# First units of a fused attention, mixing and expert kernel: weights converted 512 columns at a time with a mask made on POOL

## The chip, the cores and the metric

The kernel runs on one core of a Trainium2 chip. TensorE (PE) does the matrix products, VectorE (DVE), ScalarE (ACT) and GpSimd (POOL) the elementwise work, and SyncE (SP) issues most loads. The metric is device time in microseconds; the time before is the median of three executions. The rows shown come from one profiled execution.

## The reference

Three layers follow one another; the weights of the second arrive as 64-bit floats.

```python
# 1. attention in chunks of 64: q, k, v are (8, 8, 576, 64)
attn = softmax(scale * q_c @ k_c.T); x = attn @ v_c          # -> (8, 576, 512)
# 2. channel mixing
xk = mu_k * x + (1.0 - mu_k) * x_prev                        # x_prev: x one token earlier
xr = mu_r * x + (1.0 - mu_r) * x_prev
k = np.maximum(xk @ w_k, 0.0)                                # w_k (512, 1024), float64
v = k * k @ w_v                                              # w_v (1024, 512), float64
r = 1.0 / (1.0 + np.exp(-(xr @ w_r)))                        # w_r (512, 512), float64
x = r * v
# 3. four causal attention experts, two of them chosen per token by a gate
```

## The kernel before, in words

Each float32 operand of a product is split in a high and a low part, and each product is three matmuls (`mm3`, L51 to L59). The first two layers (`attn_mix`) go over 12 units of 384 tokens. Of a unit, PE does 48 matmuls for r (`mix_r`), 96 for k (`mix_k`), 96 for v (`mix_v`). Between them stand the steps of attention (`attend`): transposes of q and k (L126), scores `Sps` (L153), softmax on DVE and ACT (L158 to L167), transposes of the probabilities, and `PVps` (L183). One block of scores covers two tiles of 128 tokens.

**Conversion.** The weights are read as pairs of 32-bit words (`st`) and turned into float32 by shifts and masks: `conv`, 256 columns at a time, 40 pieces: 8 of w_r, 16 of w_k, 16 of w_v. For a piece SP issues a load of 256 KB; ACT squares the high word read as a float (L297, to find values too small); DVE runs L298, L299, L300, and with L302 multiplies by the outcome of the comparison; then `split` copies the high part on ACT (L314) and POOL subtracts (L315) for the low part. There are three buffers `st`, two of `cb`, two of `cz`.

**Shift.** For each unit and each 128 channels, `s_shift` builds xr and xk: POOL takes the difference of a token and the one before (L226), DVE multiplies and adds (L235), ACT copies the high part (L236), and the low part (L237) is a subtraction, on POOL in units 0 and 1 and on DVE later.

**What sets the order.** The functions are called in an order written out by hand (`CFG["first"]`, `CFG["pro"]`, `CFG["early"]`); a list scheduler then fixes the order on each engine, and each engine takes its instructions in that order. All 40 pieces are converted while the first unit is worked on. In the third layer (`experts`) nothing is edited.

Of the kernel before, what the change touches and what calls it, by code (L numbers as in the profile page):

```python
# [8 lines left out]
F32 = mybir.dt.float32  # L9
# [13 lines left out]
CFG = dict(ps=(2, 3, 1, 2), P=5, sm=3, load=6, lag=(3, 4), out=(5, 1), qk1=(1, 1), qk0=(10, 1.2), v=(11, 1), order=(3, 4, 0, 1, 2), after=1, conv='v', clo='g', x2hi='g', x2lo='v', ylo='g', yhi='v', xt='aa', r2='av', klo='vg', slo='gv', d='gg', amul='vg', nearly=2, x2b=1, yb=4, qb=4, direct=((0, 1), (1, 1), (1, 1)), tailAV=4, kp=1, yt=1, yf=2, zb=1, om=(4, 3, 2, 1, 0), hp=1000, x2d=2, early=3, rate0=0.43, rate=0.45, sh=(10, 12, 2), sh2=(11, 1, -1), pro=(17, 0.56, 20, 14), alag=2, seq=0, end=2, outL=(10, 2), outE=2, first='qqcvcvcv', kcp='aa', dsc='v', ldb=2, vb=3, cn=256, stb=3, xb=4, pa=5, tb=2, first_j=7, cb=2)  # L23
# [10 lines left out]
def eng(nc, c):  # L34
    return nc.vector if c == "v" else nc.gpsimd
# [26 lines left out]
def attn_mix(tc, at, x2T, q, k, v, mu_k, mu_r, w_k, w_v, w_r, ident, attended_all, mixed_k):  # L62
# [14 lines left out]
    with ExitStack() as ctx:  # L77
# [12 lines left out]
        mu = wkr.tile([128, 2, KD], F32, name="mu")  # L90

# [51 lines left out]
        def s_S(j):  # L143
# [19 lines left out]
            z = at.tile([128, 2 * H], F32, tag="z", name="z")  # L163
# [3 lines left out]
            eng(nc, CFG["amul"][2 * j // TPU >= CFG["nearly"]]).tensor_tensor(  # L167
# [53 lines left out]
        def s_shift(u, ws, g):  # L221
            x = XT[u]
            now, prev = x[:, g, :, 1:], x[:, g, :, :SEG]
            late = u >= CFG["nearly"]
            d = wkr.tile([128, NSEG, SEG], F32, tag="xa", bufs=2, name="xa")
            eng(nc, CFG["d"][late]).tensor_tensor(d, now, prev, op=ALU.subtract)  # L226
            for w in ws:
                nm = "kr"[w]
                if g == 0:
                    XS[u, w] = Split(wkr.tile([128, KD, UNIT], F32R, tag="xh" + nm, name="xh" + nm),  # L230
                                     wkr.tile([128, KD, UNIT], F32R, tag="xl" + nm, name="xl" + nm))
                o = XS[u, w]
                a = d if w == ws[-1] else wkr.tile([128, NSEG, SEG], F32, tag="r2", bufs=2, name="xb")
# [126 lines left out]
        for c in CFG["first"] + "q" * (CFG["ldb"] - 2) + "v" * (CFG["vb"] - 3):  # L360
# [9 lines left out]
        steps, rate, rest, at0 = CFG["pro"]  # L370
        credit = 0.0
        for i in range(steps):
            attend(2)
            credit += rate
            while credit >= 1:
# [4 lines left out]
        convert(rest)  # L380
        if steps <= at0:
            attended(0)
            first_shift()
# [29 lines left out]
def expert_weights(tc, at, w_gate, wq, wk, wv):  # L413
# [467 lines left out]
```

## Time and profile before

| | |
|---|---|
| three runs | 1073.24 us median (1073.1 to 1078.78) |
| profiled execution | 1074.6 us, of which the span of the trace is 1072.8 us |
| PE busy over the span | 1004.7 us (94%) |
| DVE, ACT, POOL busy | 749.8, 586.0, 448.0 us |
| PE busy in the first five of 40 slices | 4, 6, 7, 8, 6 tenths |
| DVE busy in the same slices | 4, 9, 9, 9, 9 tenths |

A slice is 26.8 us. A busy digit is the share of a slice; 9 is 90% or more. After the sixth slice PE is at 9 but for the end. The duration of one instruction holds its own waiting inside the engine, and neighbours on one engine overlap by some tens of nanoseconds, so sums of durations slightly exceed the time covered.

### The profile page before, as it was taken

How to read it: one execution, taken by the hardware profiler on the slowest of the kernel's cores; microseconds unless marked ns; L12 is line 12 of the kernel's file. 1: busy time of each engine (PE TensorE's matmuls, PEld its weight loads, DVE VectorE, ACT ScalarE, POOL GpSimd, SP SyncE). 2: the span in 40 equal slices, each digit the busy share in tenths (PEclk: the TensorE clock that was granted, in tenths of full speed). 3: DMA queues.
4: the chain of work that ended last, by engine and by line, in shares of the span. 5: the costliest groups of instructions: out<-in, count | busy, mean ns of one | idle time of the engine just before them, and what ended most of it. 6: DMA issues, size and time to landing. Idle time of an engine off the chain costs nothing.

```text
span 1072.8 us, 22466 instructions
## 1 busy us (share of the span) xinstructions
PE 1004.7 (94%) x8422; PEld 959.2 (89%) x8422; DVE 749.8 (70%) x1853; ACT 586.0 (55%) x1413; POOL 448.0 (42%) x550
## 2 busy tenths in 40 slices
PE   4678689999999999999999999999999999999997
PEld 3567579999899999999999999999999898999985
DVE  4999984562765665575666542498787687878996
ACT  4647547254454535464534323367776666766674
POOL 1485652453654555464644544534331233323101
PEclk9779799999999999999999999999999999999999
DMA  8735462223333232424021222662642535254212
GB/s 190 197 93 139 120 165 53 59 57 84 79 90 90 70 85 60 115 59 119 22 70 40 69 60 63 136 175 60 156 143 64 161 71 165 64 154 123 83 53 71
DMA packets 170404, 105.29 MB, mean 98 GB/s; under 512 B 133832, under 2 KB 146232, under 8 KB 170296
## 3 DMA queue, kind: packets, MB, share of 16 engines
q1 hardware_dynamic: 134904, 54.56, 20.4%
q0 software_dynamic: 35392, 49.30, 17.8%
q8 instruction: 67, 1.10, 0.5%
q14 instruction: 41, 0.34, 0.1%
HBM read 66.01 MB, written 28.38 MB: 88 GB/s over the span
## 4 chain that ended last, share of the span: by engine, by line
PE 64%; DVE 21%; DMA 5%; ACT 4%; issue 4%; SPq 2%; POOL 1%; ACTq 0%; DVEq 0%; POOLq 0%
PE mps L57 12%; PE mps L59 12%; PE mps L58 12%; PE pj L57 5%; PE pj L58 4%; PE pj L59 4%; PE Tps L656 3%; PE AVps L680 2%; PE Tps L126 2%; DVE cb L299 2%; DVE xa L235 2%; PE AVps L676 2%; PE Sps L596 2%; PE Sps L595 2%; DVE cz L302 2%
## 5 line engine op out<-in xcount | busy, mean ns | idle before, releaser
L57 PE MATMUL mps<-kh,wvh 128*128 128x384 f32 x384 | 131.8, 347 | 8.4 <-ACT wvh L314 7.3
L57 PE MATMUL mps<-xhk,wkh 128*128 128x384 f32 x384 | 132.9, 346 | 2.8 <-ACT r L257 2.8
L226 POOL TENSOR_TENSOR xa<-XT 128x384 f32<-128x384 f32 x96 | 95.1, 999 | 88.8 <-DVE xlr L237 46.8
L58 PE MATMUL mps<-kl,wvh 128*128 128x384 f32 x384 | 129.5, 339 | 2.1 <-POOL kl L266 2.1
L58 PE MATMUL mps<-xlk,wkh 128*128 128x384 f32 x384 | 130.3, 339 | 0.0
L59 PE MATMUL mps<-xhk,wkl 128*128 128x384 f32 x384 | 130.0, 339 | 0.0
L59 PE MATMUL mps<-kh,wvl 128*128 128x384 f32 x384 | 128.9, 340 | 0.2
L264 DVE TENSOR_TENSOR r<-r 128x384 f32<-128x384 f32 x80 | 68.6, 858 | 83.1 <-ACT r L257 83.0
L266 POOL TENSOR_TENSOR kl<-r,kh 128x384 fp32r<-128x384 f32 x80 | 87.8, 1102 | 82.1 <-ACT kh L265 81.1
L608 ACT ACTIVATE P<-sm,nm 128x128 f32<-128x128 f32 (+4 forms) x160 | 91.3, 571 | 35.4 <-DVE nm L598 20.1
L235 DVE SCALAR_TENSOR_TENSOR xa<-xa,mu,XT 128x384 f32<-128x384 f32 x96 | 85.8, 907 | 15.1 <-POOL xa L226 15.1
L598 DVE CUSTOM_DVE_ANT_0 sm<-Sps,mask 128x192 f32<-128x192 f32 (+3 forms) x192 | 83.6, 438 | 15.5 <-PE Sps L596 13.7
L265 ACT ACTIVATE kh<-r 128x384 fp32r<-128x384 f32 x96 | 50.3, 524 | 62.2 <-DVE r L264 61.8
L656 PE MATMUL Tps<-ident,P 128*128 128x128 f32 x480 | 81.0, 273 | 2.3 <-DVE P L617 0.9
L57 PEld LDWEIGHTS mps<-kh,wvh 128*128 128x128 f32 x384 | 72.8, 190 | 11.1 <-ACT wvh L314 8.4
L517 POOL DMA_DIRECT2D K<-Kp x64 | 34.1, 546 | 111.6 <-ACT Kp L510 111.0
L57 PE MATMUL mps<-xhr,wrh 128*128 128x384 f32 x192 | 67.3, 353 | 11.5 <-ACT sig L250 4.6
L57 PEld LDWEIGHTS mps<-xhk,wkh 128*128 128x128 f32 x384 | 73.2, 191 | 4.1 <-ACT r L257 3.6
L58 PEld LDWEIGHTS mps<-kl,wvh 128*128 128x128 f32 x384 | 73.1, 190 | 3.4 <-POOL kl L266 3.3
L59 PEld LDWEIGHTS mps<-kh,wvl 128*128 128x128 f32 x384 | 72.6, 190 | 1.2 <-POOL wvl L315 1.0
L58 PEld LDWEIGHTS mps<-xlk,wkh 128*128 128x128 f32 x384 | 73.1, 190 | 0.1
L59 PEld LDWEIGHTS mps<-xhk,wkl 128*128 128x128 f32 x384 | 72.9, 190 | 0.0
(197 smaller groups left out, 2939.7 us busy)
## 6 DMA issues: line engine op xcount, KB each, us to landing
x2T<-x2d POOLq DMA_DIRECT2D x48, 384.0 KB, 3.4
x<-x2T POOLq DMA_DIRECT2D x32, 576.0 KB, 6.1
ldv<-in_v_dram SPq DMA_DIRECT2D x144, 64.0 KB
K<-Kp POOLq DMA_DIRECT2D x64, 144.0 KB, 3.0
ldq<-in_q_dram SPq DMA_DIRECT2D x32, 256.0 KB
ldk<-in_k_dram SPq DMA_DIRECT2D x32, 256.0 KB
out_dram<-o SPq DMA_DIRECT2D x32, 256.0 KB
st<-in_moe_w_k_dram SPq DMA_DIRECT2D x16, 256.0 KB
```

What stands on the lines that cost most here:

```text
L57: nc.tensor.matmul(out=out, lhsT=ah, rhs=bh, start=first and i == 0, stop=False)
L58: nc.tensor.matmul(out=out, lhsT=ah, rhs=bl, start=False, stop=False)
L59: nc.tensor.matmul(out=out, lhsT=al, rhs=bh, start=False, stop=last and i == n - 1)
L226: eng(nc, CFG["d"][late]).tensor_tensor(d, now, prev, op=ALU.subtract)
L235: nc.vector.scalar_tensor_tensor(a, d, mu[:, w, g:g + 1], prev, op0=ALU.mult, op1=ALU.add)
L264: eng(nc, CFG["r2"][u >= CFG["nearly"]]).tensor_tensor(r2, r, r, op=ALU.mult)
L265: nc.scalar.activation(out=o.hi, in_=r2, func=ACTF.Copy)
L266: eng(nc, CFG["klo"][u >= CFG["nearly"]]).tensor_tensor(o.lo, r2, f32(o.hi), op=ALU.subtract)
L517: nc.gpsimd.dma_start(out=d[half[j]], in_=t[half[i]])
L598: nc.vector.tensor_tensor_reduce(out=sm[:n, a:a + w], in0=pp[:n, :w], in1=mk[:, a:a + w], op0=ALU.add, op1=ALU.min, scale=-scale, scalar=3e38,
L608: nc.scalar.activation(out=x[:n, :nk], in_=sm[:n, :nk], func=ACTF.Exp, scale=-1.0, bias=nm[:n, :1], accum_out=z)
L656: nc.tensor.transpose(pp[:, j - j0], x[:, o:o + 128], ident)
```

## The change

Weights go through in 20 pieces of 512 columns (`cn=512`), 4 of w_r, 8 of w_k, 8 of w_v, 512 KB each. The comparison moves to POOL, which turns the square into a word that is zero or a mask (one `tensor_scalar` with one tensor operand); DVE's first instruction ands it in, so three DVE instructions remain, and the buffer `cb` goes. The low part of the weights is subtracted on DVE (`clo='v'`). There are two buffers `st` instead of three; the first four pieces use the not yet used buffers of the shifted x. In units 0 to 2 (`dact=3`) ACT computes (1 - mu) * x_prev, DVE adds mu * x, and DVE also subtracts the low part; POOL takes differences from unit 3 on. The normalising multiplication of the softmax (`amul`) stays on DVE for score blocks 0 to 6, where it was 0 to 2. The order of stages becomes `first='qqcvvcc'`, `pro='aaacaaaaacccaaaaaasacc'` (a: a step of attention, c: a piece, s: the first shift), `early=(2, 1)`. `vb` goes from 3 to 2, and the expert weights take other buffers that have come free; of the three `st` buffers one held such a weight, so the output tiles, which share the tag, had two and have two.

```diff
@@ s_shift
-            late = u >= CFG["nearly"]
-            d = wkr.tile([128, NSEG, SEG], F32, tag="xa", bufs=2, name="xa")
-            eng(nc, CFG["d"][late]).tensor_tensor(d, now, prev, op=ALU.subtract)
+            by_act = u < CFG["dact"]
+            if not by_act:
+                d = wkr.tile([128, NSEG, SEG], F32, tag="xa", bufs=2, name="xa")
+                nc.gpsimd.tensor_tensor(d, now, prev, op=ALU.subtract)
...
-                nc.vector.scalar_tensor_tensor(a, d, mu[:, w, g:g + 1], prev, op0=ALU.mult, op1=ALU.add)
+                m = mu[:, w, g:g + 1]
+                if by_act:
+                    nc.scalar.activation(out=a, in_=prev, func=ACTF.Copy, scale=mu1[:, w, g:g + 1])
+                    nc.vector.scalar_tensor_tensor(a, now, m, a, op0=ALU.mult, op1=ALU.add)
+                else:
+                    nc.vector.scalar_tensor_tensor(a, d, m, prev, op0=ALU.mult, op1=ALU.add)
                 nc.scalar.activation(out=o.hi[:, g], in_=af, func=ACTF.Copy)
-                eng(nc, CFG["slo"][late]).tensor_tensor(o.lo[:, g], af, f32(o.hi[:, g]), op=ALU.subtract)
+                nc.vector.tensor_tensor(o.lo[:, g], af, f32(o.hi[:, g]), op=ALU.subtract)
@@ conv
-            st = at.tile([128, n, 2], I32, tag="st", bufs=CFG["stb"], name="st")
+            i = done[0] - 1
+            if i < 4:
+
+                st = wkr.tile([128, n, 2], I32, tag=("xhr", "xlr", "xhk", "xlk")[i], name="st")
+            else:
+                st = at.tile([128, n, 2], I32, tag="st", bufs=CFG["stb"], name="st")
...
-            b = at.tile([128, n], I32, tag="cb", bufs=CFG["cb"], name="cb")
             z = at.tile([128, n], F32, tag="cz", bufs=2, name="cz")
+            b = z.bitcast(I32)
+
             nc.scalar.activation(out=z, in_=f32(h), func=ACTF.Square)
-            nc.vector.tensor_scalar(b, h, 3, 0x3FFFFFF8, op0=ALU.logical_shift_left, op1=ALU.bitwise_and)
+            nc.gpsimd.tensor_scalar(z, z, F64_SMALL * F64_SMALL, 2.0 - 2.0 ** -20, op0=ALU.is_ge, op1=ALU.mult)
+            nc.vector.scalar_tensor_tensor(b, h, 3, b, op0=ALU.logical_shift_left, op1=ALU.bitwise_and)
             nc.vector.scalar_tensor_tensor(b, l, 29, b, op0=ALU.logical_shift_right, op1=ALU.bitwise_or)
             nc.vector.scalar_tensor_tensor(b, h, -(1 << 30), b, op0=ALU.bitwise_and, op1=ALU.bitwise_or)
-            if nth(CFG["conv"], done[0]) == "v":
-                nc.vector.scalar_tensor_tensor(z, z, F64_SMALL * F64_SMALL, f32(b), op0=ALU.is_ge, op1=ALU.mult)
...
             split(z, dst, g, c0, n)
```

On DVE, early in the program, where w_r's and w_k's pieces alternate with the softmax of the second block of scores (`cb`, `cz`: a piece; `m`, `z`, `P`: the softmax). Before:

```order
L298 TENSOR_SCALAR cb<-st 128x256 x2
L299 SCALAR_TENSOR_TENSOR cb<-st,cb 128x256 x2
L300 SCALAR_TENSOR_TENSOR cb<-st,cb 128x256 x2
L302 SCALAR_TENSOR_TENSOR cz<-cz,cb 128x256 x2
L298 TENSOR_SCALAR cb<-st 128x256
L299 SCALAR_TENSOR_TENSOR cb<-st,cb 128x256
L300 SCALAR_TENSOR_TENSOR cb<-st,cb 128x256
L302 SCALAR_TENSOR_TENSOR cz<-cz,cb 128x256
L158 TENSOR_REDUCE m<-Sps 128x8 x2
```

Now, at the same place (L312 to L314 are the three instructions of a piece, L324 its low part):

```order
L312 SCALAR_TENSOR_TENSOR cz<-st,cz 128x512
L313 SCALAR_TENSOR_TENSOR cz<-st,cz 128x512
L314 SCALAR_TENSOR_TENSOR cz<-st,cz 128x512
L312 SCALAR_TENSOR_TENSOR cz<-st,cz 128x512
L324 TENSOR_TENSOR wrl<-cz,wrh 128x512
L313 SCALAR_TENSOR_TENSOR cz<-st,cz 128x512
L314 SCALAR_TENSOR_TENSOR cz<-st,cz 128x512
L159 TENSOR_REDUCE m<-Sps 128x8 x2
```

A piece of 512 columns is three conversions and one subtraction on DVE, and the conversion of the next piece starts ahead of the subtraction of the last. Up to the last piece DVE has 80 such instructions, where it had 160 of 256 columns.

On POOL, over the conversion of w_r and the first pieces of w_k. Before:

```order
L315 TENSOR_TENSOR wrl<-cz,wrh 128x256 x8
L214 MEMSET XT 128x4
L217 COPY XT<-XT 128x4
L315 TENSOR_TENSOR wkl<-cz,wkh 128x256 x3
L226 TENSOR_TENSOR xa<-XT 128x384 x2
L217 COPY XT<-XT 128x4
L315 TENSOR_TENSOR wkl<-cz,wkh 128x256
L237 TENSOR_TENSOR xlr<-xa,xhr 128x384
```

Now (L311 makes the mask; COPY moves the last token of a unit, and waits for the attention):

```order
L311 TENSOR_SCALAR cz<-cz 128x512 x7
L215 MEMSET XT 128x4
L218 COPY XT<-XT 128x4
L311 TENSOR_SCALAR cz<-cz 128x512 x2
L218 COPY XT<-XT 128x4
L311 TENSOR_SCALAR cz<-cz 128x512 x2
L218 COPY XT<-XT 128x4
L311 TENSOR_SCALAR cz<-cz 128x512 x5
```

All instructions with two tensor operands are gone from POOL here; 20 masks have come.

On PE, at the end of v of unit 0, where it takes the last piece of w_v (`mps` with its number is one bank of 384 results; `kh_1367` before and `kh_1102` now are the last of eight blocks of k). Before:

```order
L57 MATMUL mps_1482<-kh_1367,wvh_91 128x384
L58 MATMUL mps_1482<-kl_1368,wvh_91 128x384
L57 MATMUL mps_1530<-kh_1367,wvh_91 128x384
L58 MATMUL mps_1530<-kl_1368,wvh_91 128x384
L126 MATMUL Tps_2467<-ident_60,ldq_2068 128x128 x4
L126 MATMUL Tps_2474<-ident_60,ldk_2070 128x128 x4
L59 MATMUL mps_1482<-kh_1367,wvl_92 128x384
L59 MATMUL mps_1530<-kh_1367,wvl_92 128x384
```

Now:

```order
L57 MATMUL mps_1187<-kh_1102,wvh_91 128x384
L58 MATMUL mps_1187<-kl_1103,wvh_91 128x384
L59 MATMUL mps_1187<-kh_1102,wvl_92 128x384
L59 MATMUL mps_1228<-kh_1072,wvl_92 128x384
L57 MATMUL mps_1228<-kh_1102,wvh_91 128x384
L58 MATMUL mps_1228<-kl_1103,wvh_91 128x384
L59 MATMUL mps_1228<-kh_1102,wvl_92 128x384
L127 MATMUL Tps_1996<-ident_60,P_1703 128x128 x3
L127 MATMUL Tps_2217<-ident_60,ldq_1819 128x128 x4
L127 MATMUL Tps_2224<-ident_60,ldk_1821 128x128 x4
L57 MATMUL mps_1276<-kh_820,wvh_91 128x384
L58 MATMUL mps_1276<-kl_821,wvh_91 128x384
```

Before, two banks end with two matmuls each behind the last piece, and the fourth bank and 12 of unit 1's 48 matmuls of r are done by then. Now three banks take each piece together; behind the last piece stand 11 matmuls of them, 11 transposes, the 24 matmuls of the fourth bank (mps_1276) and all 48 of unit 1's r. From unit 1's k on, PE's order is the same in both but for a few places where neighbours change.

## Rows read from the trace of the kernel before

**Rows 1.** The page's head, busy engines and 40 slices of the span.

```profile
span 1072.8 us, 22466 instructions
PE 1004.7 (94%) x8422; PEld 959.2 (89%) x8422; DVE 749.8 (70%) x1853; ACT 586.0 (55%) x1413; POOL 448.0 (42%) x550
...
PE   4678689999999999999999999999999999999997
...
DVE  4999984562765665575666542498787687878996
...
GB/s 190 197 93 139 120 165 53 59 57 84 79 90 90 70 85 60 115 59 119 22 70 40 69 60 63 136 175 60 156 143 64 161 71 165 64 154 123 83 53 71
```

**Rows 2.** Windows: length, then PE, PEld, DVE, ACT, POOL busy; clock; DMA.

```profile
9.00:155.00 146.00, 102.16 (x1187) 89.20 (x1181) 136.62 (x239) 81.41 (x185) 79.26 (x88) 0.84 0.60 150
160.00:180.00 20.00, 20.00 (x117) 20.00 (x116) 8.16 (x13) 15.27 (x31) 6.49 (x10) 1.00 0.32 80
```

**Rows 3.** Waits of PE, 60 to 160 us: total, times, longest.

```profile
PE mps L57 <- ACT wvh L314: 7.3, 3, 3.3
```

**Rows 4.** Timeline: first and last piece on DVE, last on POOL, unit 1's k.

```profile
9.23 0.29 DVE L298 TENSOR_SCALAR cb<-st 128x256 int32<-128x256 int32 x1 [9.23 <-DMA st<-in_moe_w_r_dram]
...
154.06 0.41 DVE L302 SCALAR_TENSOR_TENSOR cz<-cz,cb 128x256 f32<-128x256 f32 x1
...
155.00 0.73 POOL L315 TENSOR_TENSOR wvl<-cz,wvh 128x256 fp32r<-128x256 f32 x1 [1.47 <-ACT wvh L314]
...
165.80 0.34 PE L57 MATMUL mps<-xhk,wkh 128*128 128x384 f32 x1
```

**Rows 5.** Groups of DVE by form, 0 to 160 us: busy, mean ns, idle before.

```profile
L299 DVE SCALAR_TENSOR_TENSOR cb<-st,cb 128x256 int32<-128x256 int32 x40 | 28.7, 726 | 0.5
L302 DVE SCALAR_TENSOR_TENSOR cz<-cz,cb 128x256 f32<-128x256 f32 x40 | 25.3, 644 | 2.3 <-ACT cz L297 1.7
L300 DVE SCALAR_TENSOR_TENSOR cb<-st,cb 128x256 int32<-128x256 int32 x40 | 23.6, 599 | 0.3
L298 DVE TENSOR_SCALAR cb<-st 128x256 int32<-128x256 int32 x40 | 17.2, 433 | 12.8 <-DMA st<-in_moe_w_r_dram 11.0 <-DMA st<-in_moe_w_k_dram 1.4 <-DMA st<-in_moe_w_v_dram 0.3
...
L158 DVE TENSOR_REDUCE m<-Sps 128x8 f32<-128x512 f32 x14 | 9.0, 680 | 0.0
```

**Rows 6.** Chain of waits, 0 to 180 us: start, us, what.

```profile
25.05 0.67 DVE cb L299 x2
...
27.06 0.22 DVE cb L298
...
30.89 0.60 DVE P L159
...
40.78 5.76 DMA st<-in_moe_w_k_dram
...
47.32 1.13 DVE z L164
...
89.74 0.53 DVE xa L235
...
94.65 0.47 DVE kl L266
```

**Rows 7.** Groups of POOL by form, 9.2 to 154.5 us.

```profile
L226 POOL TENSOR_TENSOR xa<-XT 128x384 f32<-128x384 f32 x18 | 18.0, 1008 | 4.6 <-ACT XT L44 4.3
L315 POOL TENSOR_TENSOR wkl<-cz,wkh 128x256 fp32r<-128x256 f32 x16 | 14.0, 881 | 12.1 <-ACT wkh L314 12.1
```

**Rows 8.** Groups of POOL by form, 300 to 1072 us.

```profile
L707 POOL TENSOR_TENSOR Yl<-Yf,Yh 128x512 fp32r<-128x512 f32 x14 | 18.3, 1305 | 13.2 <-DVE Yh L46 12.8 <-DVE Y0h L46 0.3
...
L46 POOL CAST x2d<-x2o 128x384 fp32r<-128x384 f32 x32 | 16.7, 535 | 37.2 <-DVE x2o L281 21.6 <-DMA x2T<-x2d 10.8 <-DVE wv L436 4.8
```

**Rows 9.** A group of ACT by form, 0 to 160 us.

```profile
L297 ACT ACTIVATE cz<-st 128x256 f32<-128x256 f32 x40 | 17.2, 435 | 7.9 <-DMA st<-in_moe_w_r_dram 3.0 <-POOL wvl L315 2.0 <-POOL wrl L315 1.0
```

More of the change, by code (lines that the diff above doesn't have):

```diff
@@ L22 @@
 UNIT = 384
-CFG = dict(ps=(2, 3, 1, 2), P=5, sm=3, load=6, lag=(3, 4), out=(5, 1), qk1=(1, 1), qk0=(10, 1.2), v=(11, 1), order=(3, 4, 0, 1, 2), after=1, conv='v', clo='g', x2hi='g', x2lo='v', ylo='g', yhi='v', xt='aa', r2='av', klo='vg', slo='gv', d='gg', amul='vg', nearly=2, x2b=1, yb=4, qb=4, direct=((0, 1), (1, 1), (1, 1)), tailAV=4, kp=1, yt=1, yf=2, zb=1, om=(4, 3, 2, 1, 0), hp=1000, x2d=2, early=3, rate0=0.43, rate=0.45, sh=(10, 12, 2), sh2=(11, 1, -1), pro=(17, 0.56, 20, 14), alag=2, seq=0, end=2, outL=(10, 2), outE=2, first='qqcvcvcv', kcp='aa', dsc='v', ldb=2, vb=3, cn=256, stb=3, xb=4, pa=5, tb=2, first_j=7, cb=2)
+CFG = dict(ps=(2, 3, 1, 2), P=5, sm=3, load=6, lag=(3, 4), out=(5, 1), qk1=(1, 1), qk0=(10, 1.2), v=(11, 1), order=(3, 4, 0, 1, 2), after=1, conv='v', clo='v', x2hi='g', x2lo='v', ylo='g', yhi='v', xt='aa', r2='av', klo='vg', amul='vg', nearly=2, x2b=1, yb=4, qb=4, direct=((0, 1), (1, 1), (1, 1)), tailAV=4, kp=1, yt=1, yf=2, zb=1, om=(4, 3, 2, 1, 0), hp=1000, x2d=2, early=(2, 1), dact=3, rate0=0.43, rate=0.45, sh=(10, 12, 2), sh2=(11, 1, -1), pro='aaacaaaaacccaaaaaasacc', alag=2, seq=0, end=2, outL=(10, 2), outE=2, first='qqcvvcc', kcp='aa', dsc='v', ldb=2, vb=2, cn=512, stb=2, xb=4, pa=5, tb=2, first_j=7)
 SEG = 192
@@ L324, in attn_mix @@
                 nc.gpsimd.dma_start(out=mu[:, w], in_=src.rearrange("(k p) -> p k", p=128))
+        nc.gpsimd.tensor_scalar(mu1, mu, -1.0, 1.0, op0=ALU.mult, op1=ALU.add)
         AHEAD = CFG["xb"]
@@ L359, in attn_mix @@
         loads = {"q": iter(range(CFG["ldb"])), "v": iter(range(CFG["vb"]))}
-        for c in CFG["first"] + "q" * (CFG["ldb"] - 2) + "v" * (CFG["vb"] - 3):
+        for c in CFG["first"] + "q" * (CFG["ldb"] - 2) + "v" * (CFG["vb"] - 2):
             if c == "c":
@@ L368, in first_shift @@
                     s_shift(0, ws, g)
[L370 to L375, printed above, removed]
+        for c in CFG["pro"]:
+            if c == "a":
+                attend(2)
+            elif c == "c":
                 convert(1)
-                credit -= 1
-            if i == at0:
+            else:
+                attended(0)
                 first_shift()
[L380 to L383, printed above, removed]
         credit = 0.0
@@ L423, in expert_weights @@
             if nm == "v" or g % 2 == 0:
-                two = [at.tile([128, 512], F32R, tag=t, bufs=CFG["stb"] if t == "st" else CFG["vb"] if t == "ldv" else CFG["ldb"] if t[:2] == "ld" else CFG["tb"] if t in ("qT", "kT", "PT") else 2, name=f"w{nm}")
-                       for t in (tags.pop(), tags.pop())]
+                t = tags.pop()
+                if t == "P":
+                    two = at.tile([128, 1024], F32R, tag=t, bufs=2, name=f"w{nm}")
+                    two = [two[:, :512], two[:, 512:]]
+                else:
+                    two = [at.tile([128, 512], F32R, tag=t, bufs=2, name=f"w{nm}") for _ in range(2)]
             h, l = two if nm == "v" or g % 2 == 0 else (x[:, n:] for x in two)
```

14 lines of the change are left out of this document (6 added, 8 removed).

## The prediction

> **What bounds the kernel now.** I read the page's slices first. Over the whole span PE is busy 94%, and from the seventh slice on its digit is 9; the gaps lie in the first six slices, some 155 us, where DVE's digit is 9 from the second to the fifth and 8 in the sixth [rows 1]. So whatever the change does elsewhere hides behind PE, and its worth is decided in that stretch. The window of 9 to 155 us says the same in numbers: DVE is busy 136.6 of 146 us, PE 102.2 with a mean granted clock of 0.84, POOL 79.3; in 160 to 180 us PE is busy throughout at clock 1.00, with 117 matmuls in 20 us, 0.171 us each [rows 2]. The waits then say what PE lacks: its longest after 60 us are for the converted w_v [rows 3]. The timeline marks the end of the conversion: the first instruction of a piece on DVE at 9.23, the last at 154.06, the last low part from POOL at 155.00 plus 0.73, that is 155.7, and unit 1's k starts on PE at 165.80 [rows 4]. Behind that point PE's order is nearly the same in both kernels and PE is full. So the change is worth what it moves unit 1's k: that is the quantity to forecast.
>
> The groups of DVE say why conversion takes so long. L299, L300 and L302 are the same size, but take 726, 599 and 644 ns, and L298 433 [rows 5], while the chain of waits has two L299 in 0.67, so 0.335 each, and an L298 in 0.22 where nothing disturbs them [rows 6].
>
> **DVE's work, undisturbed.** Prices from the chain [rows 6]: 0.335 for 256 columns with two inputs, 0.22 for L298 and the small ones, 0.60 for 512 columns, 1.13 for 1024, 0.53 for a shift, 0.47 for a subtraction of 384.
>
> Before, up to the last piece: 120 x 0.335 + 40 x 0.22 = 49.0; softmax of six blocks and a bit, 26 x 0.60 + 9 x 1.13 + 12 x 0.22 = 28.4; 18 shifts, 9.5; 8 low parts of k and 4 outputs of 384, 5.7. Sum 92.6.
>
> Now: 20 pieces x 4 x 0.60 = 48.0. The 512 column price is that of a subtraction with an input in PSUM; 0.335 plus 256 more columns at the slope from 0.335 to 0.60 would give the same. Softmax of six blocks, all their multiplications now on DVE: 6 x (4 x 0.60 + 2 x 1.13 + 2 x 0.22) = 30.6. Shifts 18 x 0.53 + low parts 16 x 0.47 = 17.1, of which 7.5 came from POOL. Low parts of k 3.8. Sum 99.5: DVE's own work does not fall, it rises by 7.
>
> **The stretch.** Busy time before is 136.6 against 92.6, so DVE loses 44 us to something in its instructions. POOL is busy 79.3 us in the same window [rows 2], almost all with subtractions of two operands [rows 7], so each microsecond of POOL costs DVE 0.55. The group that reads PSUM alone, L158, is at 680 ns against 0.60, hardly stretched [rows 5, 6]; so it is sharing with POOL, not a slower engine. Up to the last piece POOL is left with 20 masks. The trace has no mask; it has a one operand copy of 384 at 535 ns, 0.71 at 512 columns, and a two operand subtraction of 512 at 1305 ns [rows 8]. I take 0.9, nearer the copy, as the mask has one tensor operand: 18 us of POOL, 10 us of stretch. Bounds: 7.5 at 0.71; 14.5 at 1.3; 0 if one operand work disturbs nothing; 26 if each mask blocks DVE for all of a 1.3.
>
> The Trainium skill (SBUF — State Buffer, section Who interferes with whom) says that a DVE instruction with two SBUF inputs and a GpSimd instruction that reads SBUF exclude each other, for the whole of the one that starts first. The row of L158 agrees. By that rule it does not help that the mask has one operand, only that POOL works less; in full the masks would cost up to 26 instead of 10, and the result would be the third rival below.
>
> **Start and idle time.** The first piece is now 512 KB: 256 KB more at 190 GB/s [rows 1] is 1.4 us, the square about 0.6 (435 ns at 256 columns [rows 9]), the mask 0.9: DVE starts at 9.2 + 2.9 = 12.2 with hops. Before, 9.4 us of the window were idle [rows 2]. What comes in: a piece goes ACT, POOL, DVE, ACT, DVE with two buffers `cz`; DVE waits for each mask with all its softmax and shifts behind it; from the seventh piece on a load waits on SP for one of two buffers, behind loads of q, k and v that wait for PE; POOL's copies of the last token, which wait for the attention, stand ahead of masks. I take 11 us; 7.5 if waits are as now, 20 if each of seven turns of the two buffers leaves 2 us uncovered. Loading a piece took 5.76 us from issue [rows 6].
>
> ACT gains 18 scalings of 384 and loses half of its per-instruction cost in the pieces; at 81 of 146 us [rows 2] it hides them, and if not, DVE's waits grow, which the 20 holds.
>
> **The sum.** 12.2 + 99.5 + 10 + 11 = 132.7 for the last low part of w_v, against 155.7. Behind it PE has more to do: 11 matmuls, 11 transposes, 24 matmuls of the fourth bank, 48 of unit 1's r, 94 in all x 0.171 = 16.1, against the measured 165.8 - 155.7 = 10.1. The larger piece costs here, since now three banks wait for each piece. Unit 1's k then starts at 148.8, 17.0 earlier. What follows keeps its order and its work, but for a few instructions: shifts of unit 2 add ACT and DVE work while PE is full; at 15.3 and 8.2 of 20 us busy [rows 2] they have room. The profiled execution took 1074.6, its span 1072.8; 17.0 less is 1057.6, and from the median 1073.24 it is **1056**.
>
> The forecast's own range comes from 7.5 to 20 of idle and 7.5 to 15 of stretch: the last piece at 126.7 to 146.7, the time 1050 to 1070.
>
> **Rivals.**
>
> *The pieces stay ahead of DVE.* The large pieces are fewer, and DVE always has softmax and shifts to fill in: idle 3, stretch 6. Last piece at 120.7, unit 1's k at 136.8, 29 earlier: 1044. For it speaks that DVE waited less than 2 us for loads after the first pieces [rows 5]; against it, the longer path of a piece.
>
> *The mask blocks as much as what it replaces.* Stretch 26, last piece at 148.7, unit 1's k at 164.8, 1 us earlier: 1072. For it speaks that L298, with one input, is stretched too, from 0.22 to 433 ns [rows 5, 6]; against it, that POOL's time falls from 79 to at most 26, and even now a microsecond of POOL costs 0.55. It is what the skill's lock gives if DVE always meets it at its start.
>
> *The buffers turn too slowly (the slower side).* The place is SP's load of a piece, from the seventh on. In the forecast a buffer turns in 2 x (132.7 - 12.2) / 20 = 12 us. A turn is landing, square, mask and three conversions; with landing at twice 5.76 it is 11.5 + 0.6 + 0.9 + 1.8 = 14.8 us, and queueing on SP behind a load that waits for PE comes on top. Each microsecond over 12 costs 7, for seven turns. At 14.4 the gain is gone; from 15.2 the kernel is slower by over 0.5%; at 17 the last piece comes at 168, and the time is 1091. Against it: the first 26.8 us moved 190 GB/s, 512 KB in 2.8 us [rows 1], and later slices are slacker.
>
> **How the numbers follow.** Chances: forecast 0.64, pieces ahead 0.13, mask blocks 0.12, slow turns 0.11, of which about 0.07 beyond the point of slower. What can be told from no change is 0.5%, 5.4 us. Faster by more: the first two but for the forecast's upper edge, and a little of the third, 0.79; slower 0.07; the same 0.14. The range goes from the second case to the edge of the third: 1043 to 1071.
>
> **What would show it.** Right: no DVE group of 512 columns far above 0.65 to 0.8 us; POOL busy some 20 us in the first 130; the last low part of w_v near 133; unit 1's k near 149; PE's later slices unchanged. Each term has its row: start of the first piece, DVE busy and idle time to the last piece, the mask's mean, the 94 matmuls behind it. Wrong: if DVE idles over 20 us waiting for loads or masks, if the mask is over 1.3 us, if a two input conversion stays at twice its price with POOL nearly idle, or if unit 1's k moves and the end does not.

## The result

The changed kernel takes **1059.41 us** (median of four executions, 1058.0 to 1060.84) against 1073.17 of the kernel before on the same chip: a ratio of 0.986, 95% interval 0.983 to 0.990. The forecast was 1056, the range 1043 to 1071.

The page of the changed kernel: the head, busy engines, and slices of the span with the granted clock.

```profile
span 1056.2 us, 22240 instructions
...
PE 995.0 (94%) x8422; PEld 951.2 (90%) x8422; DVE 715.6 (68%) x1793; ACT 592.1 (56%) x1397; POOL 406.9 (39%) x487
...
PE   4679799999999999999999999999999999999997
...
DVE  4899844547653756674656632687888787878896
```

The span is 16.6 us shorter. PE executes the same 8422 matmuls, and its digits differ from [rows 1] where the conversion is, in the first six slices. DVE reaches 9 in fewer of them. Windows of the changed kernel: length, then PE, PEld, DVE, ACT and POOL busy with their instructions, clock, share of the DMA engines, GB/s.

```profile
9.00:155.00 146.00, 110.81 (x1330) 99.58 (x1323) 118.29 (x195) 98.29 (x193) 49.98 (x37) 0.93 0.65 161
...
12.36:129.37 117.01, 82.56 (x1088) 72.40 (x1084) 103.96 (x171) 82.31 (x161) 42.55 (x26) 0.91 0.69 172
```

In the first, the same stretch as in [rows 2], DVE is busy 18 us less and POOL 29 less. The second runs from the first piece to the last low part of w_v. Those two ends and unit 1's k, in the timeline of the changed kernel (start, duration, line, operation; in brackets what it waited for):

```profile
12.36 0.69 DVE L312 SCALAR_TENSOR_TENSOR cz<-st,cz 128x512 int32<-128x512 int32 x1 [12.36 <-POOL cz L311]
13.09 0.69 DVE L313 SCALAR_TENSOR_TENSOR cz<-st,cz 128x512 int32<-128x512 int32 x1
...
128.68 0.69 DVE L324 TENSOR_TENSOR wvl<-cz,wvh 128x512 fp32r<-128x512 f32 x1 [0.69 <-ACT wvh L323]
...
145.72 0.34 PE L57 MATMUL mps<-xhk,wkh 128*128 128x384 f32 x1
```

The last low part is done at 129.4 instead of 155.7 [rows 4], and unit 1's k starts 20.1 us earlier. Groups of the changed kernel by form, DVE and POOL, 0 to 130 us: busy, mean ns of one, idle time before and what ended it.

```profile
L311 POOL TENSOR_SCALAR cz<-cz 128x512 f32<-128x512 f32 x20 | 42.5, 2123 | 70.7 <-ACT cz L310 70.5
L314 DVE SCALAR_TENSOR_TENSOR cz<-st,cz 128x512 int32<-128x512 int32 x20 | 14.0, 698 | 0.2
L313 DVE SCALAR_TENSOR_TENSOR cz<-st,cz 128x512 int32<-128x512 int32 x20 | 13.9, 697 | 0.2
L312 DVE SCALAR_TENSOR_TENSOR cz<-st,cz 128x512 int32<-128x512 int32 x20 | 13.9, 695 | 14.0 <-POOL cz L311 13.9
```

The surprise is the first line: a mask takes 2.12 us, over twice what was forecast. Yet DVE's instructions of twice the columns take about what those of half the size took in [rows 5]. How a mean of 695 ns fits the 0.60 us of the forecast is seen in a stretch of DVE's timeline, here of the run e8 below, in which POOL has no mask:

```profile
69.62 0.69 DVE L313 SCALAR_TENSOR_TENSOR cz<-st,cz 128x512 int32<-128x512 int32 x1
70.22 0.17 DVE L166 TENSOR_SCALAR m<-m 128x16 f32<-128x16 f32 x1
```

The next instruction starts 0.60 after, while the record says 0.69: records overlap by some 0.09 us. So a mean of 0.69 is an undisturbed instruction of 512 columns, and sums of durations overstate an engine's time; a chain's steps, and busy time in a window, do not. The next instruction here does not read what the first one wrote. Where it does, there is no overlap: in the timeline of the changed kernel above, L313 reads the result of L312 and starts 0.73 us after it.

### The profile page after: what moved, and what is told of

Same layout as the page of the kernel before. It is cut to its first block, busy times and chain, and to the rows that moved or that the text cites. A ratio compares the mean times of both kernels' runs of the same rounds, so it can differ in the third digit from the quotient of the medians.

```text
span 1056.2 us, 22240 instructions
## 1 busy us (share of the span) xinstructions
PE 995.0 (94%) x8422; PEld 951.2 (90%) x8422; DVE 715.6 (68%) x1793; ACT 592.1 (56%) x1397; POOL 406.9 (39%) x487
## 4 chain that ended last, share of the span: by engine, by line
PE 70%; DVE 13%; ACT 7%; DMA 5%; issue 2%; POOL 1%; SPq 1%; ACTq 0%; DVEq 0%; POOLq 0%
PE mps L57 13%; PE mps L59 13%; PE mps L58 13%; PE pj L57 5%; PE pj L58 5%; PE pj L59 5%; PE Tps L665 3%; PE Tps L127 3%; PE AVps L689 2%; PE AVps L685 2%; PE Sps L605 2%; PE Sps L604 2%; DVE sm L607 1%; DMA st<-in_moe_w_v_dram 1%; DMA out_dram<-o 1%
## 5 line engine op out<-in xcount | busy, mean ns | idle before, releaser
L57 PE MATMUL mps<-xhk,wkh 128*128 128x384 f32 x384 | 131.9, 344 | 3.6 <-ACT r L264 3.6
L58 PE MATMUL mps<-xlk,wkh 128*128 128x384 f32 x384 | 129.4, 337 | 0.0
L59 PE MATMUL mps<-xhk,wkl 128*128 128x384 f32 x384 | 129.0, 336 | 0.0
L59 PE MATMUL mps<-kh,wvl 128*128 128x384 f32 x384 | 127.2, 336 | 1.2 <-DVE wvl L324 1.1
L228 POOL TENSOR_TENSOR xa<-XT 128x384 f32<-128x384 f32 x72 | 72.0, 1008 | 90.2 <-DVE xlr L244 37.9
L526 POOL DMA_DIRECT2D K<-Kp x64 | 34.5, 554 | 111.7 <-ACT Kp L519 111.2
L242 DVE SCALAR_TENSOR_TENSOR xa<-xa,mu,XT 128x384 f32<-128x384 f32 x72 | 64.2, 906 | 15.9 <-POOL xa L228 15.9
## 6 DMA issues: line engine op xcount, KB each, us to landing
K<-Kp POOLq DMA_DIRECT2D x64, 144.0 KB, 3.1
```

The source lines that it names most:

```text
L57: nc.tensor.matmul(out=out, lhsT=ah, rhs=bh, start=first and i == 0, stop=False)
L58: nc.tensor.matmul(out=out, lhsT=ah, rhs=bl, start=False, stop=False)
L59: nc.tensor.matmul(out=out, lhsT=al, rhs=bh, start=False, stop=last and i == n - 1)
L228: nc.gpsimd.tensor_tensor(d, now, prev, op=ALU.subtract)
L242: nc.vector.scalar_tensor_tensor(a, d, m, prev, op0=ALU.mult, op1=ALU.add)
L526: nc.gpsimd.dma_start(out=d[half[j]], in_=t[half[i]])
```

## The experiments

Each was timed on a chip together with the kernel before (medians 1073.6 to 1075.1 there). Unless said otherwise an edit is to the changed kernel, which was itself timed only in the first comparison, so runs are held against it by their ratios. The marks are the end of the last low part of w_v and the start of unit 1's k, in the profiled execution; the matmuls are PE's from that start to the end (before: 7129).

| kernel | median us | ratio to before, 95% interval | last low part | unit 1's k | matmuls from there on | span |
|---|---|---|---|---|---|---|
| changed | 1059.41 | 0.9862 (0.9825 to 0.9900) | 129.4 | 145.7 | 7135 | 1056.2 |
| e1 low parts on POOL | 1060.31 | 0.9875 (0.9857 to 0.9893) | 137.8 | 152.4 | 7005 | 1058.4 |
| e2 before, POOL's subtractions on DVE | 1068.13 | 0.9944 (0.9923 to 0.9965) | 153.1 | 162.4 | 6975 | 1068.2 |
| e3 differences on POOL | 1062.12 | 0.9890 (0.9870 to 0.9910) | 132.8 | 149.3 | 7143 | 1059.3 |
| e4 mask with one operation | 1059.96 | 0.9869 (0.9848 to 0.9889) | 128.6 | 148.6 | 7135 | 1060.0 |
| e5 three load buffers | 1073.69 | 0.9999 (0.9982 to 1.0016) | 114.8 | 135.6 | 7429 | 1070.4 |
| e6 256 columns | 1065.06 | 0.9917 (0.9896 to 0.9938) | 156.0 | 166.0 | 6968 | 1065.3 |
| e7 unit 2's differences on POOL | 1060.73 | 0.9885 (0.9857 to 0.9913) | 133.3 | 149.6 | 7135 | 1062.5 |
| e8 mask on DVE | 1056.71 | 0.9843 (0.9815 to 0.9871) | 128.3 | 144.6 | 7135 | 1057.3 |
| e9 loads parked early | 1058.18 | 0.9850 (0.9828 to 0.9872) | 118.8 | 137.6 | 7291 | 1053.9 |
| e10 e8 and e9 together | 1051.71 | 0.9785 (0.9759 to 0.9810) | 108.8 | 129.0 | 7439 | 1049.7 |
| e11 stages in an order like before | 1061.62 | 0.9871 (0.9848 to 0.9894) | 130.4 | 146.7 | 7135 | 1056.2 |
| e12 two operand work in the mask's place | 1060.82 | 0.9873 (0.9848 to 0.9899) | 127.2 | 144.0 | 7328 | 1058.3 |

One caution on the marks. On DVE, e7 executes the same 171 instructions between first piece and last low part as the changed kernel, busy 104.4 us against 104.0; still its last low part comes 3.9 us later, with a granted clock of 0.87 against 0.91 in that window. Marks three or four us apart are not told apart by one profile.

**e1, low parts on POOL.**

```diff
-clo='v'
+clo='g'
```

> The changed kernel with the low parts of the weights subtracted on POOL again: 20 two operand subtractions of 512, some 1.3 us each, 26 us of POOL, and 12 us less work on DVE. Theory (two operand work on POOL is what stretches DVE): the three conversions rise from 0.70 us to 0.85 or more, about 14 us of stretch eat the 12 us, the last low part of w_v comes at 128 to 133 instead of 129.4, and the time is 1057 to 1064 against 1059. Rival (DVE's own amount of work sets the end): conversions stay at 0.70, the last piece comes 10 us earlier, the time is about 1050.

Groups of e1 by form, 0 to 139 us.

```profile
L312 DVE SCALAR_TENSOR_TENSOR cz<-st,cz 128x512 int32<-128x512 int32 x20 | 20.3, 1016 | 19.7 <-POOL cz L311 19.7
L313 DVE SCALAR_TENSOR_TENSOR cz<-st,cz 128x512 int32<-128x512 int32 x20 | 16.3, 817 | 0.3
...
L324 POOL TENSOR_TENSOR wkl<-cz,wkh 128x512 fp32r<-128x512 f32 x8 | 12.0, 1504 | 10.2 <-ACT wkh L323 10.2
...
L168 DVE TENSOR_TENSOR P<-P,m 128x1024 f32<-128x1024 f32 x7 | 11.0, 1564 | 0.2
```

DVE is rid of 20 subtractions, 12 us at 0.60, and is yet busy 111.7 us up to the last low part instead of 104.0. It does a softmax block more in that time, 4.5 us by the forecast's prices, so 96.5 would be left and the stretch is 15 us more, 0.5 for each of the 30 us of two operand work that came to POOL (L324). The rival that DVE's own amount sets the end falls. The last low part, at 137.8, is later than the 128 to 133 that were expected, since that block stands ahead of it. Unit 1's k is 6.7 us later, the span's end only 2.2: 130 matmuls fewer are left behind the mark, so it isn't a clean one when the scheduler deals anew.

**e2, the kernel before with POOL's subtractions on DVE.**

```diff
-clo='g', slo='gv', d='gg'
+clo='v', slo='vv', d='vg'
```

> The kernel before with the same order by hand and 256 columns, but the low parts of the weights, the differences and low parts of the shift in units 0 and 1 on DVE instead of POOL: about 29 us more work on DVE (40 x 0.335, 18 x 0.47, 16 x 0.47). Theory (two operand work on POOL stretches DVE): L299, L300 and L302 fall from 0.73, 0.60, 0.64 to 0.42, L298 to 0.28; the last piece comes at 141 to 147 instead of 155.7, the time is 1060 to 1066. Rival (DVE's own amount of work sets the end): the last piece comes near 184, the time is about 1100.

Groups of DVE of e2 by form, 0 to 160 us, beside [rows 5].

```profile
L299 DVE SCALAR_TENSOR_TENSOR cb<-st,cb 128x256 int32<-128x256 int32 x40 | 19.7, 504 | 0.1
L302 DVE SCALAR_TENSOR_TENSOR cz<-cz,cb 128x256 f32<-128x256 f32 x40 | 16.3, 417 | 0.5
L300 DVE SCALAR_TENSOR_TENSOR cb<-st,cb 128x256 int32<-128x256 int32 x40 | 16.3, 415 | 0.2
L298 DVE TENSOR_SCALAR cb<-st 128x256 int32<-128x256 int32 x40 | 11.3, 288 | 14.9 <-DMA st<-in_moe_w_r_dram 11.2 <-DMA st<-in_moe_w_v_dram 3.2 <-DMA st<-in_moe_w_k_dram 0.5
```

DVE takes over 40 low parts and unit 0's and 1's subtractions, and is busy less (131.9 in 143.9 us) than before (136.6 in 146, [rows 2]): the same instructions fall from 726, 644, 599 and 433 to 504, 417, 415 and 288 ns. POOL is not free of two operand work in this run: four multiplications of the softmax (L167, 1905 ns each) and two differences are left up to 160 us. That part of the change alone makes the kernel 0.6% faster, some 6 us, not the 0.8 to 1.3% that was expected, and the last low part comes at 153.1, not at 141 to 147.

**e3, differences on POOL.**

```diff
-dact=3
+dact=0
```

> The changed kernel with the shift of units 0 to 2 as before on its first half: POOL takes the difference, DVE multiplies and adds, ACT doesn't scale; the low part stays on DVE. POOL gains 18 to 20 two operand differences of 1.0 us. Theory (two operand work on POOL stretches DVE): 0.55 x 20 = 11 us of stretch, shifts on DVE from 0.63 to 0.8 us; the last low part of w_v at 134 to 141, the time 1063 to 1070. Rival (ACT's waits and handoffs are what is left, and POOL costs nothing): ACT is relieved of 10 us, the last piece comes earlier, the time is 1054 to 1058.

The conversions rise to 772, 717 and 737 ns, the shift from 630 to 766. From the first piece to the last low part DVE is busy 110.8 us in 120.1, where it was 104.0 with three instructions more. The sign is the theory's, and the stretch is near it; the last low part (132.8) and the time (1062.1) fall just short of the ranges expected, the one 3.4 us later than in the changed kernel, about what one profile can't tell, the other inside its interval.

**e4, mask with one operation.** In L311 the multiplication is left out, so bits of the weights are lost.

```diff
-nc.gpsimd.tensor_scalar(z, z, F64_SMALL * F64_SMALL, 2.0 - 2.0 ** -20, op0=ALU.is_ge, op1=ALU.mult)
+nc.gpsimd.tensor_scalar(z, z, F64_SMALL * F64_SMALL, None, op0=ALU.is_ge)
```

> The changed kernel with a mask of one operation on POOL (comparison alone; the multiplication that makes the bits of the mask is left out, so the weights lose bits). Theory (the mask is a hop in the path of a piece, and its 2.1 us do not disturb DVE): the mask falls to 1.0 to 1.5 us, DVE's conversions stay at 0.70, the last piece comes 1 to 5 us earlier, the time is 1054 to 1059. Rival (each microsecond of POOL costs DVE 0.55): POOL has 12 to 22 us less, conversions get shorter than 0.70, the time falls by 7 us or more. Third: the mask is hidden, no change within 1 us.

The mask falls to 1.65 us, 9.5 us of POOL in all, and nothing follows: nearly the same conversions, last low part and time, which is the third case of the expectation. A quarter less of one operand work on POOL gives DVE nothing back. Unit 1's k is late here although the last low part isn't; the windows of e4 show what differs.

```profile
120.00:130.00 10.00, 6.85 (x30) 5.71 (x29) 8.51 (x14) 4.96 (x9) 1.49 (x1) 0.75 0.76 160
130.00:140.00 10.00, 9.52 (x168) 8.45 (x167) 7.44 (x13) 4.26 (x8) 3.63 (x6) 0.91 0.48 112
```

PE's granted clock, a mean of its two levels (1.2 and 2.4 GHz, 0.5 and 1.0 here), was 0.75 and 0.91 in these two windows, in the first of which PE was busy for 6.9 of 10 us; in the changed kernel it was 0.94 and 1.00, with PE busy for 7.5 and 10.0; and from the first piece to the last low part e4's PE did 1003 matmuls against 1088.

**e12, two operand work in the mask's place.** The square is multiplied by the high word in the place of the comparison, so bits of the weights are lost.

```diff
-nc.gpsimd.tensor_scalar(z, z, F64_SMALL * F64_SMALL, 2.0 - 2.0 ** -20, op0=ALU.is_ge, op1=ALU.mult)
+nc.gpsimd.tensor_tensor(z, z, f32(h), op=ALU.mult)
```

> The changed kernel with a POOL instruction of two operands in the mask's place: the square times the upper half of the weight, 512 columns, 20 of them (so the bits taken are not those of the weights; only the time is read). The subtractions of two operands of 512 columns that POOL did took 1.3 to 1.5 us, so some 26 to 30 us of POOL, less than the 42.5 us of one operand masks that left DVE's conversions at 0.695 us. Theory (two operand work on POOL stretches DVE, one operand work does not): the means of the three conversions rise to 0.75 to 0.95 us, DVE's busy time to the last piece from 104 to 110 or more, last piece 130 to 137, time 1058 to 1064. Rival (it was POOL's amount of work in all, or the low parts' own lateness, that made the run with low parts on POOL slower): conversions 0.69 to 0.72, last piece 126 to 130, time 1056 to 1060.

Groups of e12 by form, 0 to 130 us.

```profile
L311 POOL TENSOR_TENSOR cz<-cz,st 128x512 f32<-128x512 f32 x20 | 29.9, 1497 | 67.6 <-ACT cz L310 67.6
L314 DVE SCALAR_TENSOR_TENSOR cz<-st,cz 128x512 int32<-128x512 int32 x20 | 17.3, 865 | 0.2
...
L168 DVE TENSOR_TENSOR P<-P,m 128x1024 f32<-128x1024 f32 x5 | 7.2, 1439 | 0.1
```

With 12.6 us less of POOL than the masks, DVE is stretched: L314 by 167 ns, L168 by 150, the shifts from 630 to 772. So it is the kind of POOL instruction, two tensor operands instead of one, and not POOL's amount, that costs DVE: by these means some 9 us, about 0.3 for each microsecond of POOL. The last low part is nevertheless early, in the range of the rival, for a reason that the forecast of this run missed: in the order that the scheduler wrote for it, one score block fewer stands ahead of the last piece (10 subtractions L160 up to 130 us, where the changed kernel had 12), and DVE's busy time up to it, 104.6 us, does not rise as was expected.

**e6, 256 columns.** Twice as many pieces at each place, and

```diff
-cn=512, stb=2
+cn=256, stb=4
```

> The changed kernel with pieces of 256 columns, twice as many, four buffers, all else as it is (four output buffers in the last stage come with it, so the marks before 160 us decide). An instruction of 256 columns at 0.36 instead of half of 0.695: DVE's amount +1 to +4 us; first piece 2 to 3 us earlier; masks 40 x some 1.1 to 1.4. Theory (the three instructions and no two operand work on POOL carry the gain, the 512 columns nothing): last low part of w_v 125 to 133, unit 1's k 142 to 150, time 1055 to 1063. Rival (fixed cost of an instruction, so 512 columns carry it): each of the 160 instructions of 256 at 0.43 or more, +13 us or more, last piece over 140, time over 1067.

Groups of e6 by form, 0 to 156 us.

```profile
L312 DVE SCALAR_TENSOR_TENSOR cz<-st,cz 128x256 int32<-128x256 int32 x40 | 17.4, 436 | 18.7 <-POOL cz L311 18.7
...
L311 POOL TENSOR_SCALAR cz<-cz 128x256 f32<-128x256 f32 x40 | 49.1, 1227 | 78.7 <-ACT cz L310 77.9
```

The rival's last piece came, and its time nearly, but its reason is only a part. Between first piece and last low part DVE is busy 123.9 us in 145.1, 20 more than in the changed kernel. At 0.335 from start to start instead of 0.60 for twice the columns, 160 instructions cost 5.6 more; 16 subtractions L160 instead of 12 are two score blocks more ahead of the last piece, 10 us. Idle time is 21.2 instead of 13.0: a mask takes 1.23 us for half the columns, and the pieces wait for it (18.7, of which 10.9 is the first). So going back to 256 columns costs 5.7 us of the time, and the intervals of the two ratios overlap only at their edges. By these counts most of it comes through the mask and the order; the four output buffers came along, and no run takes these apart.

**e8, mask on DVE.**

```diff
-nc.gpsimd.tensor_scalar(z, z, F64_SMALL * F64_SMALL, 2.0 - 2.0 ** -20, op0=ALU.is_ge, op1=ALU.mult)
+nc.vector.tensor_scalar(z, z, F64_SMALL * F64_SMALL, 2.0 - 2.0 ** -20, op0=ALU.is_ge, op1=ALU.mult)
```

> The changed kernel with its mask on DVE instead of POOL, so four bit and mask instructions of 512 columns there. Price of one more two input sized instruction of 512 columns: at most 0.7 us, x 20 = 14 us of DVE work; a one operand instruction may take less, 0.3 us, 6 us in all. Theory (the mask's 2.1 us on POOL is hidden and nearly free, what counts is DVE's own amount): DVE's busy time to the last piece rises from 104 to 110 to 118, its idle falls by the 1.5 us that it waited for masks and some of the turn, last low part of w_v 134 to 142 (changed kernel: 129.4), unit 1's k 150 to 158, time 1063 to 1070. Rival (the long way ACT, POOL, DVE of a piece costs idle time, 13 us in the changed kernel): last piece 126 to 130, time 1056 to 1060.

The theory fell: DVE does 20 instructions more and the last low part comes as early. Its mask and the window from the first L312 to the last low part:

```profile
L311 DVE TENSOR_SCALAR cz<-cz 128x512 f32<-128x512 f32 x20 | 8.4, 424 | 12.6 <-ACT cz L310 12.4
```

```profile
11.13:128.27 117.14, 84.89 (x1118) 75.31 (x1119) 107.51 (x190) 83.14 (x162) 3.91 (x6) 0.90 0.68 174
```

The window holds the same instructions as that of the changed kernel and 19 masks. DVE's busy time rises by 3.5 us, not by 19 x 0.335 = 6.4, so the 42.5 us of masks on POOL had stretched it by some 3, or 0.07 for each microsecond. Its idle time falls from 13.0 to 9.6. Moving the mask to POOL was worth nothing that shows: what DVE was spared, it lost again, about half by the stretch and half by waiting.

**e5 and e9, loads earlier.** In e5 a third load buffer, with room taken from the output; in e9 pieces 5 to 12 land in w_v's own arrays, which lie idle until piece 13. Of e5, then of e9:

```diff
-stb=2, x2d=2
+stb=3, x2d=1
```

```diff
...
+            elif i < 12:
+                st = wv.park[(i - 4) // 4][:, i % 4]
...
```

> The changed kernel with three load buffers for pieces instead of two (and one instead of two output buffers of the last step of a unit, to make room; this can cost time behind 160 us, so the marks before decide). Theory (the turn of the buffers is a good part of DVE's 13 us of idle time, ACT waited 16 us for those loads): idle 7 to 10, last low part of w_v 123 to 127 (changed kernel 129.4), unit 1's k 139 to 143. Rival (loads wait but DVE fills in with softmax and shifts): last piece 128 to 131, unit 1's k 145 to 148.

> The changed kernel with loads for pieces 5 to 12 put into the room of w_v's two arrays (which nothing else uses before piece 13) instead of the two turning buffers; nothing else is taken away. Three buffers had pulled the last low part of w_v from 129 to 114.8 us and unit 1's k from 146 to 136, but with one output buffer less behind, which hid what it is worth. Theory (the buffers' turn holds the pieces back; the room that was taken for the third buffer cost the time behind 160 us): last piece 115 to 124, unit 1's k 133 to 142, and the end follows: 1047 to 1056. Rival (pieces that come earlier only push softmax behind them, and PE lacks it later): last piece as early, unit 1's k earlier by 4 us or more, but the end at 1057 to 1062, with PE's idle time behind 150 us up by as much.

In the changed kernel ACT's longest waits up to 130 us are for loads (total, times, longest):

```profile
ACT cz L310 <- DMA st<-in_moe_w_v_dram: 6.4, 3, 4.2
...
ACT cz L310 <- DMA st<-in_moe_w_k_dram: 5.4, 3, 3.6
```

With loads earlier the last low part comes 15 and 11 us sooner, so the turn of two buffers did hold the pieces back. About half of that is idle time of DVE that is gone (5.8 and 7.6 us are left of 13.0); the rest is softmax that now stands behind the last piece (10 subtractions L160 are ahead of it in both runs, not 12). The time did not follow. In e5 PE waits behind the mark for the outputs that lost a buffer (in the changed kernel the first of these waits is 2.5, and the second does not occur):

```profile
PE mps L57 <- DVE x2o L288: 8.5, 5, 2.6
PE pj L57 <- DMA x<-x2T: 5.2, 4, 2.9
```

In e9 nothing was taken away, and of the 8.1 us of unit 1's k 2.3 are left at the end, as the rival had it. The window of e9 from unit 1's k on, and below it the changed kernel from the start to that mark and from there on:

```profile
137.58:1053.90 916.32, 894.63 (x7291) 861.95 (x7290) 606.30 (x1615) 506.89 (x1232) 355.00 (x442) 1.00 0.34 89
```

```profile
0.00:145.72 145.72, 105.46 (x1289) 93.01 (x1290) 113.35 (x186) 93.08 (x178) 52.78 (x47) 0.93 0.70 172
145.72:1056.20 910.48, 889.52 (x7135) 858.19 (x7134) 602.21 (x1607) 499.00 (x1219) 354.17 (x440) 1.00 0.34 88
```

PE has 156 matmuls more to do behind the mark, 5.1 us: the pieces overtook softmax, and PE does what belongs to it later. Its idle time there, by which the rival explained the loss, is up by only 0.7.

**e10, both.** The edit of e8 on top of that of e9.

> The same with the mask on DVE (0.33 us from start to start in the run that had it there), as the candidate for the fastest. Theory (both gains add): 1 to 3 us below the run with parked loads alone. Rival (with loads early DVE is full again, so 20 x 0.33 = 6.6 us of masks now count): 3 to 7 us above it.

At 1051.71 us this is the fastest, 2.15% below the kernel before; its interval lies clear of the changed kernel's. Both expectations missed: it is 6.5 us below e9. By the medians the two gains do more than add; each by itself is inside the changed kernel's interval, so how they add is not shown. That the mask is better on DVE once the loads come early is clear of the intervals. Windows of e10, from 10.9 us, inside its first piece, to the last low part, then from unit 1's k on:

```profile
10.90:108.80 97.90, 67.24 (x707) 61.03 (x708) 92.74 (x167) 68.92 (x135) 1.27 (x3) 0.88 0.65 175
```

```profile
129.02:1049.70 920.68, 899.15 (x7439) 866.17 (x7438) 611.63 (x1625) 513.35 (x1244) 355.40 (x442) 1.00 0.35 91
```

DVE idles 5.2 us instead of 13.0, and two score blocks more stand behind the last piece (8 subtractions L160 are ahead of it, not 12). Unit 1's k is 16.7 us earlier than in the changed kernel, 9.6 of it is PE's work pushed behind the mark, and 6.5 reach the end.

**e7, unit 2's differences.**

```diff
-dact=3
+dact=2
```

> The changed kernel with unit 2's differences on POOL again, and so no scaling of unit 2 on ACT (4 of 384 or so fewer in a row). Of the 20.1 us by which unit 1's k came earlier only 16.6 reached the end. Theory (ACT's and DVE's extra work for unit 2 takes it back, PE waited 3.5 us for ACT's r in 250 to 356 us): PE's wait for r at 251 to 258 goes, time 1056 to 1058. Rival (the phase of the softmax against k's stage moved, not the scalings; the same wait stands at 349 to 356 us, where no scaling is): waits stay, time 1059 to 1061. Up to unit 1's k nothing moves, 129 and 146.

PE's wait that the changed kernel has and the kernel before hasn't stands unchanged in e7 (168 to 1050 us):

```profile
PE mps L57 <- ACT r L264: 3.5, 6, 0.7
```

So it isn't ACT's scalings of unit 2, and the theory falls. The rival's phase of the softmax was not tested by itself.

**e11, the old order of stages.**

```diff
-pro='aaacaaaaacccaaaaaasacc'
+pro='aaaacaaaacaaaacaaaaacccccccs'
```

> The changed kernel with its first units written in an order like that before: softmax steps first with few pieces between, then seven pieces in a row, then unit 0's shift. Theory (the order in which the program is written is nearly washed out, since each engine's instructions are put in order by when they are ready, and by the first 160 rows of DVE's order only the names of a few k parts differ): last piece 127 to 132, time 1057 to 1062. Rival (the new order carries part of the gain): last piece over 134, time over 1063.

As the theory had it: the marks move by a microsecond, the time not beyond its interval. The scheduler decides the order; the written one hardly enters, in the one other order that was tried.

## Why the prediction was right

The time fell within the forecast's own range, and its steps can be held against the marks. DVE was the bound, and two operand work on POOL did stretch it; but that the numbers came out so near is in part luck, as errors of opposite sign met.

- *Where it is decided.* Right. PE's matmuls behind unit 1's k are as many as before (7135, 7129).
- *Start of the first piece.* 12.2 forecast (its terms, 9.2 + 2.9, give 12.1), 12.36 measured, by luck. ACT's square starts at 9.63, 0.4 us later than the first instruction before [rows 4], where 1.4 were set for the larger load; the first mask takes 1.94 instead of 0.9.

```profile
9.63 0.67 ACT L310 ACTIVATE cz<-st 128x512 f32<-128x512 f32 x1 [0.62 <-DMA st<-in_moe_w_r_dram]
10.39 1.94 POOL L311 TENSOR_SCALAR cz<-cz 128x512 f32<-128x512 f32 x1 [2.99 <-ACT cz L310]
```

- *DVE's own work, 99.5, and the stretch, 10.* Nearly right in sum, 5.5 us too high, and wrong inside. DVE was busy 104.0, so by the forecast's prices the stretch is 4.5, of which e8 puts some 3 down to the masks. In what is left lies a term that the prices lack: 11 times a conversion stands right behind the one of the same piece that it needs, at some 0.72 us instead of 0.60. The mask was mis-sized both ways, and the two errors offset each other: 2.12 us on POOL instead of 0.9, and 0.07 of stretch for each microsecond (e8) instead of 0.55. That price, taken from the kernel before, belongs to two operand work: e1 gives 0.5, e12 0.3. (The bounds of 7.5 and 14.5 us are 7.8 and 14.3 by their own terms. And 726 or 433 ns against 0.335 or 0.22 us sets durations against steps from start to start: undisturbed, the durations are 0.41 and 0.29 [rows 4]. The 44 us of stretch before come from busy time and are not touched by it.)
- *Idle time, 11.* Measured 13.0. What ended it, in the changed kernel from 12 to 130 us:

```profile
DVE cz L312 <- POOL cz L311: 13.9, 4, 12.4
DVE m L165 <- ACT P L163: 3.5, 3, 1.6
DVE xb L240 <- ACT xb L239: 2.8, 3, 1.6
DVE wvl L324 <- ACT wvh L323: 2.3, 2, 1.6
```

  The 12.4 is the first piece; only 1.5 are for masks. In e8, with no mask on POOL, idle time is 3.4 us less all the same, and ACT's waits for loads of pieces fall from 16.3 to 9.3; that the one comes by the other, through the buffers, is argued and not shown.
- *Last low part, 132.7, and 16.1 of PE behind it.* 129.4 and 16.3, with 92 of the matmuls counted and 32 short ones of the attention (`PVps`, 0.7 us) that were not.
- *The same gain at the end.* This step failed in part: unit 1's k is 20.1 us earlier, where 17.0 were forecast, and the span ends 16.6 earlier. That 16.6 is so near to 17.0 is luck: 3 us more were gained than forecast, and 3.5 of the gain did not last. From unit 1's k on, PE is busy 889.5 us instead of 887.8 and idle 21.0 instead of 19.2; the kernel before:

```profile
0.00:165.80 165.80, 116.94 (x1294) 102.02 (x1295) 141.10 (x246) 91.79 (x203) 87.18 (x104) 0.86 0.63 151
165.80:1072.80 907.00, 887.80 (x7129) 857.14 (x7128) 608.73 (x1607) 494.24 (x1210) 360.83 (x446) 1.00 0.34 88
```

  The new waits for ACT's r are 3.5 us; why they came is open. The medians differ by 13.8 rather than 16.6, as the profiled execution of the changed kernel, 1058.0, is its fastest and that of before, 1074.6, above its median.
- *The mask blocks as much as what it replaces.* Refuted for this mask (it is the second rival, which the prediction once calls the third). The Trainium skill (SBUF — State Buffer, section Who interferes with whom) would have the lock for any GpSimd instruction that reads SBUF. Masks of 42.5 us in all left two input conversions at 695 to 698 ns, where 686 is undisturbed (e8); the measurement decides. For two operands the sign is the rule's, with a third of POOL's time lost (e12), not all.
- *Buffers turn too slowly.* The forecast's place was right, the price in time small: ACT waits for loads, and e9, with most of these waits gone, ends at about the same time.
- *Pieces ahead of DVE.* Its idle of 3 us is nearly what e10 reaches (5.2), and its price of 12 us below the forecast was too hopeful, since pieces that come early push softmax behind the mark.

*What would show it.* One of the signs of being wrong came: the mask is over 1.3 us, and POOL is busy 42.5 us up to the last piece instead of some 20. The time held because DVE lost so little to it.

What each part was worth: taking POOL's subtractions to DVE is some 6 us by itself (e2, on the kernel before), and 512 columns are 5.7 us with the order that comes with them (e6); neither is shown to be the larger. Given back to POOL one at a time, the subtractions of the changed kernel cost 1 and 3 us, inside the interval (e1, e3). The mask on POOL and the written order are worth nothing that shows (e8, e11). The softmax's multiplications on DVE, and the room for the first four pieces, no run takes by itself.

## What to carry to other kernels

Work put on another engine to spare the bounding one has to be priced as a step of its chain, not only as time taken off: the mask on POOL saved DVE some 6.6 us of instructions (20 of 0.33 from start to start in e8), and stretch and waiting took them back. A stretch measured beside one kind of neighbour holds for that kind; ask how many operands the neighbour reads. And a mark in mid-kernel is worth its distance only if as much work is left behind it: count PE's matmuls from there to the end.

## What was not expected of the hardware

- POOL took 2.12 us for a one operand `tensor_scalar` of 512 columns with two operations, 1.65 with one (e4), 1.23 for 256 columns with two (e6), and 1.50 for a two operand product of 512 (e12). The copy of 384 columns in [rows 8] at 0.535 was a bad neighbour to price it by. DVE did the same mask in 0.42.
- A DVE instruction of 512 columns that reads the result of the one just ahead starts some 0.72 us after it (12.36 and 13.09 in the timeline above), and 0.60 after one whose result it doesn't need.
- Of the 16.6 us of span, 9.7 are PE's busy time with the same 8422 matmuls (1004.7, 995.0): up to unit 1's k it needs 105.5 us for 1289 of them at a granted clock of 0.93, before 116.9 for 1294 at 0.86. That PE's slower matmuls before lay in time that it would else have waited for DVE is our reading; no run separates the two.
